# Program order on every engine, one unit of four head pairs per block, masks from iota, a joint update of r and k, and a weight conversion without GpSimd

## Chip, cores, metric

One core of one Trainium2 chip. The metric is the device time of one execution in microseconds (us), median of several; "span" is the time from the first to the last instruction of the profiled execution, some 2 us shorter. Engines: PE = TensorE, DVE = VectorE, ACT = ScalarE, POOL = GpSimd, SP = SyncE, which issues the DMAs.

## The reference

A recurrent attention (batch 4, 8 heads, 768 tokens, head size 48) and then an MLP with exact GELU over the 3072 tokens, model size 384, hidden size 2048. The MLP's weights come as float64.

```python
for t in range(S):                                   # rwkv6_finch
    kt, vt, rt, wt = k[:, :, t], v[:, :, t], r[:, :, t], w[:, :, t]
    cur = einsum('bhd,bhe->bhde', u[None] * kt, vt)
    y[:, :, t] = einsum('bhd,bhde->bhe', rt, state + cur)
    state = wt[..., None] * state + einsum('bhd,bhe->bhde', kt, vt)   # state starts at 0 for each batch
x = y.transpose(0, 2, 1, 3).reshape(3072, 384)
h = x @ w_in
out = (0.5 * h * (1 + erf(h / sqrt(2)))) @ w_out
```

## The kernel before

The tokens go in 8 blocks of 384 (two per batch). The attention of a block is split into 11 steps ("slots"): one product of r*u and k, six levels of products with an update of r and k after each, a transpose of k, the state, y from v, y from the state. Its result goes by ten small DMAs into `xT`, the input of the block's MLP. Attention of block x runs beside the MLP of block x-1, so only the first block's attention stands alone, and it stands beside the conversion of w_in from float64.

```python
def to_float32(dst, src):                    # one piece, 128 x 512 or 128 x 384; 28 pieces
    raw = cv.tile([128, PIECE], I64, name="raw", bufs=3)[:, 0:n]
    nc.sync.dma_start(out=raw, in_=src)
    ...
    nc.scalar.activation(out=f.bitcast(F32), in_=hi.bitcast(F32), func=AF.Abs)
    nc.vector.tensor_scalar(...)             # clamp
    nc.vector.tensor_scalar(...)             # shift and mask
    nc.vector.scalar_tensor_tensor(...)      # sign
    nc.vector.tensor_scalar(...)             # exponent of the low word
    nc.vector.scalar_tensor_tensor(...)      # low word, scaled
    nc.gpsimd.tensor_add(dst, f.bitcast(F32), e.bitcast(F32))

def attention(n):                            # n = block * 2 + unit; a unit is two head pairs
    ...
    before = st_of.get(n - UB)               # state of the block before
    ...
    for h in LEVELS:                         # 1, 2, 4, 8, 16, 32
        d = products(...)                    # PE; copied into a under a mask
        ...
        nc.vector.tensor_mul(r2, r2, t2[:, :, 0:1].to_broadcast([128, nb, h]))
        nc.gpsimd.tensor_mul(k2, k2, t2[:, :, 1:2].to_broadcast([128, nb, h]))
        nc.vector.tensor_mul(new, t2[:, :, 0], t2[:, :, 1])
        yield
    ...                                      # state: 11 small DVE instructions a unit (10 in a batch's second block)
    load(n + 2 * UB)

for x in range(NX):                          # no program-order line: the scheduler orders each engine
    slots = zip(*(attention(x * UB + i) for i in range(UB)))
    if x == 0:                               # beside the 12 pieces of w_in
        spread(slots, weights(in_pieces), len(in_pieces), len(in_pieces))
    else:                                    # beside the MLP before; x == 1 converts 16 pieces of w_out too
        ...
        spread(slots, steps, n, n - 4)
```

Of the kernel before, what the change touches and what calls it, by code (L numbers as in the profile page):

```python
# [10 lines left out]
U32 = mybir.dt.uint32  # L11
U8 = mybir.dt.uint8
# [5 lines left out]
C = 64  # L18
G = 64
T = 384  # L20
# [14 lines left out]
def kernel(  # L35
# [21 lines left out]

    nc = tc.nc
    NU = rkw.shape[0]
    D = 48  # L60
    NP = u.shape[1]
    UB = NP // Q
    N_TOK, DM = out.shape
    NX = N_TOK // T
# [8 lines left out]
    io = ctx.enter_context(tc.tile_pool(name="io", bufs=4))  # L73
# [3 lines left out]
    ps = ctx.enter_context(tc.tile_pool(name="ps", bufs=1, space=PSUM))  # L77

# [3 lines left out]
    def load(n):  # L82
        if n >= NU:
            return
        x = io.tile([128, 3, Q, T], F32, name="rkw_in")
        if n < UB:
            nc.sync.dma_start(out=x[:, 0:2], in_=rkw[n, :, 0:2])
            nc.sync.dma_start(out=x[:, 2], in_=rkw[n, :, 2])
        else:
            nc.sync.dma_start(out=x, in_=rkw[n])  # L90
        y = io.tile([128, v.shape[2]], F32, name="v_in")
        nc.sync.dma_start(out=y, in_=v[n])
        loaded[n] = x, y

    u_sb = const.tile([128, NP], F32, name="u_sb")
    nc.sync.dma_start(out=u_sb, in_=u)
    for n in range(UB):
        load(n)

    ident = const.tile([128, 128], F32, name="ident")  # L100
    make_identity(nc, ident)


    masks = {}

    def mask(h, n):
        masks[h] = const.tile([128, 1, n], U8, name=f"mask{h}")
        return wk.tile([128, n], F32, name="maskf")

    m = mask(0, C)  # L110
    for p in range(2):
        nc.vector.tensor_copy(out=m[half[p]], in_=ident[half[p], half[p]])
    nc.vector.tensor_copy(out=masks[0][:, 0, :], in_=m)
    for h in LEVELS[:-1]:
        m = mask(h, C // 2)
        for p in range(2):
            mv = m[half[p]].rearrange("p (q j) -> p q j", j=h)
            nc.gpsimd.memset(m[half[p]], 1.0)
            nc.gpsimd.affine_select(out=mv, in_=mv, compare_op=ALU.is_ge, fill=0.0, base=0,
                                    pattern=[[-2 * h, C // 2 // h], [0, h]], channel_multiplier=1)  # L120
            nc.gpsimd.affine_select(out=mv, in_=mv, compare_op=ALU.is_ge, fill=0.0, base=h - 1,
                                    pattern=[[2 * h, C // 2 // h], [0, h]], channel_multiplier=-1)
        nc.vector.tensor_copy(out=masks[h][:, 0, :], in_=m)


    a_bufs = [const.tile([128, 2, NI, C], F32, name=f"a{i}") for i in range(2)]
    for a in a_bufs:
        nc.gpsimd.memset(a, 0.0)

    st_bufs = [const.tile([128, Q * NC * D + G - D], F32, name=f"st{i}") for i in range(2 * UB)]  # L130
    for s in st_bufs:
        nc.gpsimd.memset(s, 0.0)

    w_in_sb = const.tile([128, NJ, DF], F32, name="w_in_sb")
    w_out_sb = const.tile([128, NF, DM], F32, name="w_out_sb")

    def to_float32(dst, src):

        n = src.shape[1]
        raw = cv.tile([128, PIECE], I64, name="raw", bufs=3)[:, 0:n]  # L140
        nc.sync.dma_start(out=raw, in_=src)
        words = raw.bitcast(U32).rearrange("p (a b) -> p a b", b=2)
        lo, hi = words[:, :, 0], words[:, :, 1]
        f = cv.tile([128, PIECE], U32, name="f")[:, 0:n]
        e = cv.tile([128, PIECE], U32, name="e")[:, 0:n]

        nc.scalar.activation(out=f.bitcast(F32), in_=hi.bitcast(F32), func=AF.Abs)  # L147
        nc.vector.tensor_scalar(out=f.bitcast(F32), in0=f.bitcast(F32), scalar1=as_float(0x38000000),  # L148
                                scalar2=as_float(0x47EFFFFF), op0=ALU.max, op1=ALU.min)
        nc.vector.tensor_scalar(out=f, in0=f, scalar1=3, scalar2=0x3FFFFFFF,  # L150
                                op0=ALU.logical_shift_left, op1=ALU.bitwise_and)

        nc.vector.scalar_tensor_tensor(out=f, in0=hi, scalar=0xC0000000, in1=f,  # L153
                                       op0=ALU.bitwise_and, op1=ALU.bitwise_or)

        nc.vector.tensor_scalar(out=e, in0=f, scalar1=0xFF800000, scalar2=None, op0=ALU.bitwise_and)  # L156
        nc.vector.scalar_tensor_tensor(out=e.bitcast(F32), in0=lo, scalar=2.0 ** -52, in1=e.bitcast(F32),  # L157
                                       op0=ALU.mult, op1=ALU.mult)
        nc.gpsimd.tensor_add(dst, f.bitcast(F32), e.bitcast(F32))  # L159

    def weights(pieces):
        for dst, src in pieces:
            if wide:
                to_float32(dst, src)
            else:
                nc.sync.dma_start(out=dst, in_=src)
            yield
# [4 lines left out]
    def attention(n):  # L172

        x, un = divmod(n, UB)
        first = x % HALVES == 0
        rkw_in, vt = loaded.pop(n)
        r, k, w = (rkw_in[:, i].rearrange("p q t -> p (q t)") for i in range(3))
        rc, kc = (z.rearrange("p (i c t) -> p i c t", c=2, t=C) for z in (r, k))
        at = a_bufs[n % 2]
        st = st_bufs[n % len(st_bufs)]  # L180
        before = st_of.get(n - UB)
        st_of[n] = st
# [4 lines left out]

        ru = wk.tile([128, Q * T], F32, name="ru")
        for q in range(Q):
            nc.scalar.activation(out=ru[:, q * T:(q + 1) * T], in_=r[:, q * T:(q + 1) * T], func=AF.Copy,  # L190
                                 scale=u_sb[:, un * Q + q:un * Q + q + 1])
        ruc = ru.rearrange("p (i c t) -> p i c t", c=2, t=C)

        def products(right, width):
            d = ps.tile([128, 2, BANK], F32, name="d", tag="d", bufs=3)
            for i in range(NI):
                for g in range(2):
                    for p in range(2):
                        nc.tensor.matmul(d[half[p], g, i * width:(i + 1) * width],  # L199
                                         lhsT=kc[half[g], i, p], rhs=right(half[g], i, p), start=True, stop=True)  # L200
            return d[:, :, 0:NI * width]

        d = products(lambda z, i, p: ruc[z, i, p], C)
        nc.vector.copy_predicated(out=at.rearrange("p g i t -> p (g i) t"),
                                  mask=masks[0].to_broadcast([128, 2 * NI, C]), data=d)
        yield

        tots = wk.tile([128, Q * T], F32, name="tots")
        tot, at_tot = w, 0
        for h in LEVELS:  # L210
            m = C // 2 // h
            right = rc.rearrange("p i c (m two j) -> p i c m two j", two=2, j=h)[:, :, :, :, 1, :]
            d = products(lambda z, i, p: right[z, i, p], C // 2)
            to = at.rearrange("p g i (m two j) -> p (g i) m two j", two=2, j=h)[:, :, :, 1, :]
            if m == 1:
                for p in range(2):
                    s = slice(p * 64, p * 64 + h)
                    nc.scalar.copy(out=at[s, :, :, h:], in_=d[s].rearrange("p g (i t) -> p g i t", t=h))
            else:
                nc.vector.copy_predicated(  # L220
                    out=to, mask=masks[h].rearrange("p o (q j) -> p o q j", j=h).to_broadcast([128, 2 * NI, m, h]),
                    data=d)
            nb = Q * T // (2 * h)
            t2 = tot.rearrange("p (n two) -> p n two", two=2)
            r2 = r.rearrange("p (n two j) -> p n two j", two=2, j=h)[:, :, 1, :]
            k2 = k.rearrange("p (n two j) -> p n two j", two=2, j=h)[:, :, 0, :]
            nc.vector.tensor_mul(r2, r2, t2[:, :, 0:1].to_broadcast([128, nb, h]))  # L227
            nc.gpsimd.tensor_mul(k2, k2, t2[:, :, 1:2].to_broadcast([128, nb, h]))  # L228
            new = tots[:, at_tot:at_tot + nb]
            nc.vector.tensor_mul(new, t2[:, :, 0], t2[:, :, 1])  # L230
            tot, at_tot = new, at_tot + nb
# [3 lines left out]
        kt_ps = ps.tile([128, 2, BANK], F32, name="kt_ps", tag="d", bufs=3)  # L235
        for i in range(NI):
            o = (i % N3) * 128
            nc.tensor.transpose(kt_ps[:, i // N3, o:o + 128], k[:, i * 128:(i + 1) * 128], ident)  # L238
        kt = wk.tile([128, NI, 2, G], F32, name="kt")
        nc.scalar.copy(out=kt.rearrange("p (b i) g d -> p b (i g d)", b=2), in_=kt_ps[:, :, 0:N3 * 128])  # L240
        yield

        vc = [[vt[:, (i * 2 + g) * D:(i * 2 + g) * D + G] for g in range(2)] for i in range(NI)]
        kv_ps = ps.tile([128, 2, BANK], F32, name="kv_ps", tag="d", bufs=3)
        for i in range(NI):
# [169 lines left out]
```

## Time and profile before

| before | value |
|---|---|
| time, median of 4 runs (range) | 740.7 us (739.8 to 742.0) |
| span, mean granted PE clock | 740.9 us, 0.968 |
| busy: PE, DVE, ACT, POOL | 679.4, 284.6, 137.9, 151.6 us |
| first MLP's last matmul ends | 183.5 us |
| from there to the end | 557.4 us |

PE is busy 92% of the span, and of the missing 8% all but 3.4 us at the very end lie before 183.5 us (the stretches are in the prediction). What PE waits for there is the list of PE's waits, kernel before (columns: what waited, for what; total us, times, longest):

```profile
PE d L199 <- DVE rkw_in L227: 19.7, 10, 7.5
PE y_ps L268 <- DVE st L259: 16.8, 1, 16.8
PE d L199 <- ACT ru L190: 8.5, 2, 7.9
PE d L199 <- issue: 7.5, 1, 7.5
```

To be seen: DVE's updates (`rkw_in`) and DVE's state (`st`) hold PE for 36.5 us. I shall split every kernel at one place, the end of the first MLP's last matmul: **head** before it, **rest** after it.

### The profile page before, as it was taken

The numbers are of one execution on the slowest core, as the hardware profiler recorded it, in microseconds if no ns is written. First come the engines' busy times: TensorE is split into PE (matmuls) and PEld (weight loads), VectorE is DVE, ScalarE is ACT, GpSimd is POOL, SyncE is SP. The second block draws the span as 40 slices with busy tenths as digits, with TensorE's granted clock in tenths as the row PEclk, the third lists the DMA queues.
The fourth block names the chain that finished last, engine by engine and source line by source line (L and its number), as shares of the span: only waits on it lengthen the run. The fifth ranks groups of instructions, "written<-read, shape, count | busy, mean of one in ns | idle before, by whom it ended". The sixth has DMA issues, their size and how long they took to land.

```text
span 740.9 us, 20544 instructions
## 1 busy us (share of the span) xinstructions
PE 679.4 (92%) x9296; PEld 444.6 (60%) x9296; DVE 284.6 (38%) x644; ACT 137.9 (19%) x254; POOL 151.6 (20%) x166
## 2 busy tenths in 40 slices
PE   3733697899999999999999999999999999999998
PEld 2632454466666666666666666666666666665554
DVE  2999969941433034231433035121433044200000
ACT  2122232401222021301121021301120011201200
POOL 5643435400231013200330014100330023100000
PEclk9985698999999999999999999999999999999999
DMA  8145723215000510024000500033000100010000
GB/s 344 66 132 160 245 65 107 87 46 175 8 3 2 157 71 2 3 77 150 2 3 28 169 32 3 2 123 104 3 2 13 43 13 3 2 43 22 0 12 21
DMA packets 16966, 47.06 MB, mean 64 GB/s; under 512 B 2800, under 2 KB 8944, under 8 KB 15088
## 3 DMA queue, kind: packets, MB, share of 16 engines
q1 hardware_dynamic: 16880, 45.76, 18.6%
q8 instruction: 73, 1.20, 0.7%
q14 instruction: 13, 0.11, 0.0%
HBM read 36.31 MB, written 4.72 MB: 55 GB/s over the span
## 4 chain that ended last, share of the span: by engine, by line
PE 84%; DVE 10%; DMA 3%; issue 2%; POOL 1%; ACT 0%; SPq 0%; POOLq 0%; DVEq 0%
PE o_ps L320 34%; PE h_ps L311 33%; PE d L199 10%; PE y_ps L284 3%; DVE rkw_in L227 2%; DVE f L153 2%; DMA v_in<-in_v_dram 2%; PE y_ps L268 1%; PE kv_ps L248 1%; DVE f L148 1%; DVE e L156 1%; DVE e L157 1%; PE kt_ps L238 1%; DVE f L150 1%; DMA rkw_in<-in_rkw_dram 1%
## 5 line engine op out<-in xcount | busy, mean ns | idle before, releaser
L311 PE MATMUL h_ps<-xT,w_in_sb 128*128 128x384 f32 x768 | 266.0, 499 | 2.0 <-DMA xT<-ysb 2.0
L320 PE MATMUL o_ps<-w_out_sb,gt 128*128 128x384 f32 x768 | 256.4, 491 | 2.1 <-ACT gt L314 2.1
L320 PEld LDWEIGHTS o_ps<-w_out_sb,gt 128*128 128x128 f32 x768 | 144.3, 191 | 98.9 <-ACT gt L314 2.3
L311 PEld LDWEIGHTS h_ps<-xT,w_in_sb 128*128 128x128 f32 x768 | 143.5, 192 | 94.8 <-issue 3.0
L228 POOL TENSOR_TENSOR rkw_in<-rkw_in,tots 128x384 f32<-128x384 f32 x80 | 83.7, 1063 | 135.2 <-PE d L199 131.6
L199 PEld LDWEIGHTS d<-rkw_in 64*64 64x64 f32 x4608 | 82.2, 148 | 46.0 <-issue 26.4
L314 ACT ACTIVATE gt<-h_ps 128x384 f32<-128x384 f32 x128 | 62.6, 490 | 251.0 <-PE h_ps L311 251.0
L199 PE MATMUL d<-rkw_in 64*64 64x32 f32 x4608 | 88.3, 231 | 20.2 <-DVE rkw_in L227 19.7
L325 DVE COPY o_sb<-o_ps 128x384 f32<-128x384 f32 x24 | 13.4, 558 | 228.1 <-PE o_ps L320 228.1
L220 DVE COPY_PREDICATED a<-mask,d 128x384 f32<-128x384 uint8 x80 | 59.9, 749 | 102.0 <-PE d L199 101.7
L228 POOL TENSOR_TENSOR rkw_in<-rkw_in 128x384 f32<-128x384 f32 x16 | 21.0, 1333 | 294.6 <-PE d L199 294.6
L227 DVE TENSOR_TENSOR rkw_in<-rkw_in,tots 128x384 f32<-128x384 f32 x80 | 67.3, 841 | 31.1 <-PE d L199 30.2
L259 DVE SCALAR_TENSOR_TENSOR st<-st,tots,kv_ps 128x48 f32<-128x48 f32 x160 | 30.0, 259 | 33.3 <-PE kv_ps L248 33.2
L287 ACT COPY ysb<-y_ps 128x768 f32<-128x768 f32 x16 | 12.8, 797 | 142.7 <-PE y_ps L284 142.7
L190 ACT ACTIVATE ru<-rkw_in,u_sb 128x384 f32<-128x384 f32 x32 | 17.4, 604 | 93.1 <-PE d L199 78.8
L199 PE MATMUL d<-ru,rkw_in 64*64 64x64 f32 x768 | 15.8, 239 | 16.1 <-ACT ru L190 8.5
L268 PE MATMUL y_ps<-a,v_in 64*64 64x64 f32 x768 | 13.8, 226 | 16.8 <-DVE st L259 16.8
L147 ACT ACTIVATE f<-raw 128x384 f32<-128x384 f32 (+1 forms) x28 | 17.0, 608 | 56.8 <-POOL w_out_sb L159 29.7
L284 PEld LDWEIGHTS y_ps<-rkw_in,st 64*64 64x64 f32 x752 | 24.5, 144 | 4.1 <-issue 3.8
L153 DVE SCALAR_TENSOR_TENSOR f<-raw,f 128x384 uint32<-128x384 uint32 (+1 forms) x28 | 26.1, 931 | 0.2
L199 PEld LDWEIGHTS d<-ru,rkw_in 64*64 64x64 f32 x768 | 14.3, 151 | 19.7 <-issue 10.9
L284 PE MATMUL y_ps<-rkw_in,st 64*64 64x64 f32 x752 | 25.6, 229 | 0.1
(35 smaller groups left out, 259.9 us busy)
## 6 DMA issues: line engine op xcount, KB each, us to landing
rkw_in<-in_rkw_dram SPq DMA_DIRECT2D x14, 1152.0 KB, 6.2
raw<-in_w_in_dram SPq DMA_DIRECT2D x12, 512.0 KB, 3.7
raw<-in_w_out_dram SPq DMA_DIRECT2D x16, 384.0 KB, 3.0
v_in<-in_v_dram SPq DMA_DIRECT2D x16, 296.0 KB, 4.3
out_dram<-o_sb SPq DMA_DIRECT2D x24, 192.0 KB, 2.0
xT<-ysb SPq DMA_DIRECT2D x48, 72.0 KB, 3.2
rkw_in<-in_rkw_dram SPq DMA_DIRECT2D x2, 768.0 KB, 5.7
rkw_in<-in_rkw_dram SPq DMA_DIRECT2D x2, 384.0 KB, 6.1
```

The source lines that it names most:

```text
L153: nc.vector.scalar_tensor_tensor(out=f, in0=hi, scalar=0xC0000000, in1=f, op0=ALU.bitwise_and, op1=ALU.bitwise_or)
L190: nc.scalar.activation(out=ru[:, q * T:(q + 1) * T], in_=r[:, q * T:(q + 1) * T], func=AF.Copy, scale=u_sb[:, un * Q + q:un * Q + q + 1])
L199: nc.tensor.matmul(d[half[p], g, i * width:(i + 1) * width], lhsT=kc[half[g], i, p], rhs=right(half[g], i, p), start=True, stop=True)
L220: nc.vector.copy_predicated(out=to, mask=masks[h].rearrange("p o (q j) -> p o q j", j=h).to_broadcast([128, 2 * NI, m, h]), data=d)
L227: nc.vector.tensor_mul(r2, r2, t2[:, :, 0:1].to_broadcast([128, nb, h]))
L228: nc.gpsimd.tensor_mul(k2, k2, t2[:, :, 1:2].to_broadcast([128, nb, h]))
L259: nc.vector.scalar_tensor_tensor(out=stq[:, q, c], in0=stq[:, q, c - 1] if c else b4[:, q, NC - 1], scalar=totq[:, q, c:c + 1], in1=kvq[:, ...
L268: nc.tensor.matmul(y_ps[half[g], p, i * C:(i + 1) * C], lhsT=vc[i][g][half[p]], rhs=at[half[p], g, i, :], start=(i == 0), stop=True, skip_ ...
L284: nc.tensor.matmul(y_ps[half[g], c % 2, i * C:(i + 1) * C], lhsT=src[half[g], o:o + G], rhs=rc[half[g], i, c % 2], start=False, stop=True, ...
L311: nc.tensor.matmul(h_ps, lhsT=w_in_sb[:, j, f * 128:(f + 1) * 128], rhs=xT[:, j, :], start=(j == 0), stop=(j == NJ - 1))
L314: nc.scalar.activation(out=gt, in_=h_ps, func=AF.Gelu)
L320: nc.tensor.matmul(o_ps, lhsT=gs[f][:, i * 128:(i + 1) * 128], rhs=w_out_sb[:, f, :], start=(f == 0), stop=(f == NF - 1))
```

## The change

Its intent: keep DVE free of the work that delays the first block. GpSimd is taken out of the conversion and of the k update, because DVE instructions took longer beside its adds (one and the same conversion instruction took 0.41 us at 42.29, and 1.34 at 48.63, beside an add from 48.01 to 49.68 us); masks come from two iota and a few integer instructions; the four head pairs are one unit from block 2 on, so instructions are half as many and twice as wide; conversions are placed by hand (three before the state, the other 25 in the first MLP's stage); every engine keeps the source's order; loads are issued when their block is next but one.

```diff
+    ctx.enter_context(tc.manual_schedule(engines=None))     # program order on all engines
...
-        nc.gpsimd.affine_select(...)  # two per mask half, ten halves
+    nc.gpsimd.iota(row, pattern=[[0, C]], base=0, channel_multiplier=1)
+    nc.gpsimd.iota(col, pattern=[[1, C]], base=0, channel_multiplier=0)
+        nc.vector.tensor_scalar(out=s_h, in0=row[:, 0:C // 2], scalar1=sh, ..., op0=ALU.logical_shift_right)
+        nc.vector.tensor_scalar(out=m_h, in0=col[:, 0:C // 2], ...)
+        nc.vector.tensor_tensor(out=masks[h][:, 0, :], in0=s_h, in1=m_h, op=ALU.is_equal)
...
     def to_float32(dst, raw):
+        nc.scalar.activation(out=e.bitcast(F32), in_=lo, func=AF.Identity, scale=2.0 ** -51, bias=two)
         nc.scalar.activation(out=f.bitcast(F32), in_=hi.bitcast(F32), func=AF.Abs)
         nc.vector.tensor_scalar(...)  # clamp, as before
-        (shift and mask; sign; exponent; low word: four DVE instructions; add on GpSimd)
+        nc.vector.tensor_scalar(out=f, in0=f, scalar1=3, scalar2=None, op0=ALU.logical_shift_left)
+        nc.vector.scalar_tensor_tensor(out=e, in0=hi, scalar=0x80000000, in1=e,
+                                       op0=ALU.bitwise_and, op1=ALU.bitwise_or)
+        nc.vector.tensor_tensor(out=dst.bitcast(U32), in0=f, in1=e, op=ALU.add)
...
-        before = st_of.get(n - UB)
+        before = None if first else st_bufs[(x - 1) % 2]
...
-            nc.vector.tensor_mul(r2, r2, t2[:, :, 0:1].to_broadcast([128, nb, h]))
-            nc.gpsimd.tensor_mul(k2, k2, t2[:, :, 1:2].to_broadcast([128, nb, h]))
+            rk = bass.AP(...)          # r's odd halves and k's even halves in one pattern
+            nc.vector.tensor_mul(rk, rk, tt)
...
+    slots = zip(*(attention(0, unit) for unit in range(units_of(0))))
+    for slot, _ in enumerate(slots, 1):
+        if slot == N_SLOTS - 3:
+            convert(NJ)
+    load_rkw(2)
+    load_v(2)
+    for x in range(1, NX):
+        lead, last = (12, N_STEPS - 2) if x == 1 else (0, N_STEPS - 4)
+        place = [lead + (last - lead) * i // (N_SLOTS - 1) for i in range(N_SLOTS)]
+        slots = attention(x, 0)
+        for step, _ in enumerate(mlp(x - 1)):
+            while x == 1 and converted[0] < len(pieces) and (converted[0] - NJ) * 3 < (step + 1) * 4:
+                convert()
+            while place and place[0] <= step:
+                place.pop(0)
+                next(slots)
+        load_rkw(x + 2)
+        load_v(x + 2)
```

In the kernel before, PE also multiplies the first 64 tokens of a batch with a state slot of the batch before. Read in the code, that slot holds zeros: the second block of a batch fills its slots 0 to 4, and slot 5, which these products read, keeps the zeros it was set to at the start.

## The prediction

> **What bounds the kernel now.** I read three views in this order: the chain that ended last (where the bound changes), a table of stretches cut at those places, and the order of time and the groups of instructions inside the stretches that are not bound by TensorE. A "stage" below is one block of 384 tokens: its attention runs beside the MLP of the block before.
>
> First the stretches; columns are length, busy time of each engine, granted clock, DMA share and GB/s.
>
> ```profile
> 0.00:90.00 90.00, 40.88 (x1211) 36.94 (x1211) 75.32 (x143) 21.70 (x33) 45.79 (x70) 0.81 0.54 190
> 90.00:183.50 93.50, 84.56 (x915) 51.94 (x914) 57.95 (x138) 20.83 (x41) 26.52 (x25) 0.93 0.31 99
> 183.50:265.50 82.00, 82.00 (x1169) 53.21 (x1168) 25.47 (x63) 14.95 (x28) 13.27 (x12) 1.00 0.16 52
> 593.50:675.50 82.00, 82.00 (x1166) 53.49 (x1166) 22.66 (x49) 12.81 (x24) 13.26 (x12) 1.00 0.05 16
> 675.50:740.90 65.40, 61.99 (x193) 36.20 (x191) 2.23 (x4) 7.84 (x16) 0.00 (x0) 1.00 0.03 12
> ```
>
> To be seen: from 183.5 us on, PE is busy for all of each 82.0 us stage; six such stages and a last MLP make 6 x 82.0 + 65.4 = 557.4 us. No engine but PE can shorten that. Only the first 90 us (no MLP yet) and the next 93.5 us (the first MLP, 11.5 us over a full stage) can give: at best 90 + 11.5.
>
> Then what DVE does in the first 90 us, where it is busy for 75 us:
>
> ```profile
> 18.43 0.18 DVE L123 CAST mask<-maskf 128x32 uint8<-128x32 f32 x1 [0.42 <-POOL maskf L121]
> ...
> 48.63 1.34 DVE L156 TENSOR_SCALAR e<-f 128x512 uint32<-128x512 uint32 x1
> 49.88 0.25 DVE L259 SCALAR_TENSOR_TENSOR st<-st,tots,kv_ps 128x48 f32<-128x48 f32 x1
> 50.06 0.68 DVE L157 SCALAR_TENSOR_TENSOR e<-raw,e 128x512 f32<-128x512 uint32 x1
> 50.66 0.41 DVE L148 TENSOR_SCALAR f<-f 128x512 f32<-128x512 f32 x1
> 51.00 0.25 DVE L259 SCALAR_TENSOR_TENSOR st<-st,tots,kv_ps 128x48 f32<-128x48 f32 x1
> 51.17 1.33 DVE L150 TENSOR_SCALAR f<-f 128x512 uint32<-128x512 uint32 x1
> ...
> 58.64 1.60 DVE L153 SCALAR_TENSOR_TENSOR f<-raw,f 128x512 uint32<-128x512 uint32 x1
> ...
> 68.41 1.13 DVE L259 SCALAR_TENSOR_TENSOR st<-st,tots,kv_ps 128x48 f32<-128x48 f32 x6
> ```
>
> To be seen: masks come from GpSimd until 18 us though the first data is there at 6. The state recurrence, 22 small instructions, takes from 44 to 69.5 us because a conversion of w_in sits between any two steps; at the end six run in 1.13 us. The same conversion instruction takes 0.41 or 1.34 us, 0.68 or 1.60: it is held up.
>
> [...] the 1.60 us one above starts beside a GpSimd add (58.29 to 59.69 us) and ends 0.55 us after it. [...] The trace: 0.54 us for 384 contiguous elements, 0.72 at pair distance 1. [...] The trace: the 96 products of a level take 2.95 us in the first 40 us, 1.53 us in a full stage.
>
> **The change part by part.** In the built program PE has the same matmuls as before, so the PE floor stays. I use undisturbed durations of the trace, start to start where instructions follow each other.
>
> 1. Start. [...] the 17 little DVE mask instructions (about 0.15 each, as small ones in the trace) end near 10; the tot products (0.56 + 1.31 = 1.9) end at 12.2. Level 1 of both units: joint update 2 x 1.3 (768 elements at the 0.72/384 rate), copies 4 x 0.9, the second tots 1.9: 8.1, to 20.3. Level 2: 2 x 1.2 + 2 x 0.9 = 4.2, to 24.5. Three levels at about 3.1 [...], to 33.8; the last update 1.8, to 35.6. Transpose and copy of both units [...] to 38.8. Before, this point was at 42.
>
> 2. Three pieces of w_in stand in front of the state now. ScalarE's two passes (0.6 each) put the first at 40; a piece costs DVE, by starts, 0.34 + 0.34 + 0.60 and an integer add. No row shows that add; I take it as a SCALAR_TENSOR_TENSOR, 0.6. That is 1.9, up to 2.1 where one needs the result of the one before (in the trace 0.40 instead of 0.27 to the next): 2.0. So to 46.2. State 2 x 2.1 to 50.4, fences, y 2 x 2.0 [...] to 54.8, copy to 55.7, ten xT issues at 0.65 begin at 53.8, landing 2 us later: **first MLP complete in xT at 62** instead of 83.4, and PE no longer stands behind other work until 90. Gain 28 us.
>
> 3. But 25 of 28 pieces are left, where 15 were. Order on ScalarE puts the first behind the first gelu: DVE starts at 62.4 + 3 = 65.4. Up to the update of level 8, DVE has 9 pieces x 2.0 and 14 of w_out x 1.63 (0.27 + 0.27 + 0.47 + 0.5, between 1.5 and 1.77) = 40.8; tots of four units 2.6, update of 1536 elements 2.6, copies 3.6; level 2 4.1; level 4 2.6; update of level 8 1.7: 58.0 together. PE in that time has about 45 us, so **DVE sets the pace** and the point is 123.4. Then in program order about 7 us until step 19 of 28, and 30.2 us of PE that nothing hides: 8 steps x 2.68 = 21.4 and the products, transpose, kv, y and y again at 1.5 + 1.3 + 1.5 + 1.5 + 2.9.
>
> 4. The last attention step stands after step 26, so only one step (2.7 us) covers the way of y into xT, which needs about 8 (copy, ten issues, landing): 5.3 us idle. **Second MLP at 123.4 + 7 + 30.2 + 5.3 = 165.9**, before 185 (183.5 with the products that stood first). Of the 28 us, nine have been given back.
>
> 5. Full stages. GpSimd's k update (1.08 us, 12 a stage) goes into DVE, 25 us busy there, which has room. Program order costs twice: the products with u wait for ru, which stands behind the first gelu (0.6), and the second level waits for a PSUM buffer that four copies release (0.5): estimated 1.2 a stage, 7 in six. The xT way has 3 steps (8.0 us) and needs about 8: no margin. Merging level 1 with u saves next to nothing.
>
> Sum: 165.9 + 492 + 7 + 65.4 = **730 us**.
>
> **The rivals.** (a) *PE-bound stage 1.* If the conversions cost less than I think, the stage shrinks toward 82 + 5 us, and without the 1.2 us in the full stages: 62 + 87 + 492 + 65 = 706. For it: the GpSimd collisions go, 0.5 to 0.9 us each. Against it: DVE needs 58 us before PE's last 37 whatever happens to collisions, as I have already used free durations. (b) *Nothing is gained.* [...] For it: the narrow 8 us[...]. Against it: in the old stage the xT issues (7.3 us for ten) share the queue with a 1.18 MB load issued ahead; the new one issues loads after. (c) *DMA becomes the bound of stage 1.* A load of 2.96 MB for block 2 stands before the raw pieces; at 400 GB/s (seen between 5 and 20 us) it ends about 67, and the next piece is wanted at 72. If it slips, 3 to 5 us more.
>
> **Range and chances.** The start is uncertain by about 5 us, the DVE pace of stage 1 by 8, the full stages by 6: together 11, so 714 to 743, a bit wider below, as the order was evidently arranged on purpose (where attention begins in stage 1). Faster by 2% means under 725.4: 0.36. Within: 0.58. Slower: 0.06.
>
> **What would show it right or wrong.** First h_ps matmul at 57 to 67; state instructions in one run of about 4.5 us; DVE nearly always busy from 65 to 130 with PE waiting for it; a PE idle of 4 to 6 us for xT before the second MLP at 160 to 171; stages of 83 us with two short waits, for ru and for a copy. Wrong if the stages are 82.0 or above 85, if stage 1 shows PE full, if the add differs from 0.6 us, or if iota ends after 10 us.

The sum came to 730 us, and terms of it are cut: in step 1 a term for GpSimd's start, which the "near 10" still holds (the 17 mask instructions are 2.6 us of it), so that all later times hold it too. With three parentheses a cause went that no trace shows; their figures are of the kernel before's trace: 2.95 us for 96 products (beside 2 x 0.9 + 2 x 0.5 of DVE) in the levels at 3.1, 2 x 1.5 and 0.8 for transpose and copy, 2 x 2.0 for y (78 products in 4.43 us from 70.26). The 1.3 and 2.6 us of the joint updates are an estimate, scaled from 0.72 us for 384 elements (DVE's update of r, L227). Rival (b) came to some 755.

## The result, and the profile after

728.0 us (727.8 to 728.2, 4 runs) against 740.7: ratio 0.9827, 95% interval 0.981 to 0.9844, so 1.7% faster, inside the 2%. Ratios here are the mean time of one kernel's runs over the mean of the other's in the same rounds, so not quite the ratio of the medians that are quoted.

The stretches of the kernel after, cut where its bound changes (columns as in the prediction):

```profile
0.00:54.40 54.40, 31.78 (x957) 29.98 (x957) 37.85 (x90) 13.66 (x20) 4.48 (x11) 0.90 0.49 180
54.40:160.50 106.10, 92.73 (x1165) 57.24 (x1165) 70.66 (x149) 42.49 (x78) 0.00 (x0) 0.90 0.38 124
165.90:251.70 85.80, 81.74 (x1143) 53.48 (x1143) 24.15 (x44) 14.83 (x28) 0.00 (x0) 0.96 0.12 44
415.30:660.80 245.50, 245.50 (x3478) 159.82 (x3477) 80.43 (x149) 44.50 (x84) 0.00 (x0) 1.00 0.12 40
660.80:726.00 65.20, 61.90 (x192) 36.11 (x191) 2.23 (x4) 7.84 (x16) 0.00 (x0) 1.00 0.04 12
```

To be seen: the first block's attention takes 54.4 us where 90 stood, and the first MLP's stage 106.1 where 93.5 stood. The cuts are not quite alike: here the cut is at the first `h_ps` matmul (first product of an MLP), which in the kernel before started at 78.9 us; cut there, the kernel before has 78.9 + 104.6. Later stages are full of PE again, 245.5 / 3 = 81.8 us each, but the second MLP's stage has lost 4 us of PE and has a clock of 0.96. In head and rest: 160.4 + 565.6 us, against 183.5 + 557.4. **The head gained 23.1 us, the rest gave 8.2 back.**

Where the head's gain comes from, in DVE's order of time, kernel after:

```profile
42.17 0.68 DVE L205 SCALAR_TENSOR_TENSOR e<-raw,e 128x512 uint32<-128x512 uint32 x1
42.89 0.69 DVE L207 CUSTOM_DVE_ANT_0 w_in_sb<-f,e 128x1024 uint16<-128x1024 uint16 x1
43.50 0.25 DVE L322 COPY st<-kv_ps 128x96 f32<-128x96 f32 x1
43.78 1.84 DVE L327 SCALAR_TENSOR_TENSOR st<-st,tot_sb,kv_ps 128x48 f32<-128x48 f32 x10
45.54 0.25 DVE L322 COPY st<-kv_ps 128x96 f32<-128x96 f32 x1
45.82 1.84 DVE L327 SCALAR_TENSOR_TENSOR st<-st,tot_sb,kv_ps 128x48 f32<-128x48 f32 x10
47.58 0.22 DVE L343 COPY fence<-y_ps 128x2 f32<-128x2 f32 x2
62.43 0.43 DVE L202 TENSOR_SCALAR f<-f 128x512 f32<-128x512 f32 x1 [14.64 <-ACT f L201]
```

To be seen: the state, which took from 44 to 69.5 us before, now runs in one piece from 43.5 to 47.6. The uint16 line is the integer add. Then DVE has nothing to do for 14.64 us, because its next conversion waits for a ScalarE pass that stands behind the first gelu function.

Where the rest lost it, in PE's order of time, kernel after (in brackets: idle time before the line, and what ended it):

```profile
157.59 2.85 PE L391 MATMUL o_ps<-w_out_sb,gt 128*128 128x384 f32 x8
160.50 0.88 PE L382 MATMUL h_ps<-xT,w_in_sb 128*128 128x384 f32 x2
162.84 0.91 PE L382 MATMUL h_ps<-xT,w_in_sb 128*128 128x384 f32 x2 [1.46 <-DMA xT<-ysb]
165.12 0.88 PE L382 MATMUL h_ps<-xT,w_in_sb 128*128 128x384 f32 x2 [1.37 <-DMA xT<-ysb]
165.93 1.60 PE L254 MATMUL d<-rkw_in 64*64 64x32 f32 x96
167.35 0.78 PE L254 MATMUL d<-ru_sb,rkw_in 64*64 64x64 f32 x37
172.19 1.97 PE L254 MATMUL d<-ru_sb,rkw_in 64*64 64x64 f32 x59 [4.06 <-issue]
```

To be seen: two waits for `xT`, which the prediction has, and 4.06 us of "issue" in the middle of 96 equal products, which it hasn't. "issue" is time in which PE waited for nothing the profile shows. A load of 2.4 MB and one of 0.6 MB had been issued at 164.1 and 164.6 us. PE's 59 products after it take 1.97 us, where 96 take 1.61 in an undisturbed stage.

### The profile page after: what moved, and what is told of

The parts are those of the page before. It is cut to its first block, busy times and chain, and to the rows that moved or that the text cites. A ratio compares the mean times of both kernels' runs of the same rounds, so it can differ in the third digit from the quotient of the medians.

```text
span 726.0 us, 19903 instructions
## 1 busy us (share of the span) xinstructions
PE 679.7 (94%) x9248; PEld 443.8 (61%) x9248; DVE 272.1 (37%) x542; ACT 153.0 (21%) x282; POOL 4.5 (1%) x11
## 3 DMA queue, kind: packets, MB, share of 16 engines
q8 instruction: 72, 1.18, 0.7%
## 4 chain that ended last, share of the span: by engine, by line
PE 84%; DVE 10%; issue 2%; SPq 2%; DMA 1%; ACT 1%; ACTq 0%; DVEq 0%
PE o_ps L391 34%; PE h_ps L382 32%; PE d L254 11%; PE y_ps L358 3%; DVE e L205 2%; PE kt_ps L296 2%; PE y_ps L339 2%; PE kv_ps L312 1%; SPq L369 1%; DVE f L204 1%; DVE rkw_in L271 1%; DVE f L202 1%; DVE w_in_sb L207 1%; DVE w_out_sb L207 1%; DMA u_sb<-in_u_dram 1%
## 5 line engine op out<-in xcount | busy, mean ns | idle before, releaser
L271 DVE TENSOR_TENSOR rkw_in<-rkw_in,tot_sb 128x1536 f32<-128x1536 f32 (+1 forms) x45 | 71.1, 1580 | 93.7 <-PE d L254 93.6
L254 PEld LDWEIGHTS d<-rkw_in 64*64 64x64 f32 x4608 | 80.2, 146 | 38.8 <-issue 19.3
L280 DVE COPY_PREDICATED a_sb<-mask,d 128x384 f32<-128x384 uint8 x80 | 55.0, 747 | 0.0
L327 DVE SCALAR_TENSOR_TENSOR st<-st,tot_sb,kv_ps 128x48 f32<-128x48 f32 x160 | 29.0, 258 | 0.3
L254 PE MATMUL d<-ru_sb,rkw_in 64*64 64x64 f32 x768 | 17.8, 253 | 9.9 <-ACT ru_sb L234 5.0
L278 ACT COPY a_sb<-d 32x384 f32<-32x384 f32 x32 | 15.0, 469 | 38.5 <-PE d L254 37.9
L271 DVE TENSOR_TENSOR rkw_in<-rkw_in 128x1536 f32<-128x1536 f32 (+1 forms) x9 | 14.2, 1581 | 23.2 <-PE d L254 23.2
L254 PEld LDWEIGHTS d<-ru_sb,rkw_in 64*64 64x64 f32 x768 | 16.1, 162 | 10.7 <-issue 5.2
L199 ACT ACTIVATE e<-raw,two 128x384 f32<-128x384 uint32 (+1 forms) x28 | 19.6, 699 | 9.5 <-DVE w_out_sb L207 5.1
L339 PE MATMUL y_ps<-a_sb,v_in 64*64 64x64 f32 x768 | 13.8, 226 | 7.6 <-DVE st L327 7.6
L339 PEld LDWEIGHTS y_ps<-a_sb,v_in 64*64 64x64 f32 x768 | 12.6, 140 | 11.5 <-issue 11.5
```

Source lines behind the costliest of these rows:

```text
L199: nc.scalar.activation(out=e.bitcast(F32), in_=lo, func=AF.Identity, scale=2.0 ** -51, bias=two)
L254: nc.tensor.matmul(d[half[p], g, n * width:(n + 1) * width], lhsT=kc[half[g], b, i, p], rhs=right(half[g], b, i, p), start=True, stop=True)
L271: nc.vector.tensor_mul(rk, rk, tt)
L278: nc.scalar.copy(out=at[s, b, :, :, h:], in_=db[s].rearrange("p g (i t) -> p g i t", t=h))
L280: nc.vector.copy_predicated(out=at[:, b].rearrange("p g i (m two j) -> p (g i) m two j", two=2, j=h)[:, :, :, 1, :], mask=masks[h].rearran ...
L327: nc.vector.scalar_tensor_tensor(out=stq[:, qb + q, c], in0=stq[:, qb + q, c - 1] if c else b4[:, qb + q, NC - 1], scalar=totq[:, b * Q + ...
```

## The experiments

Twelve runs; the kernel before ran in each of the three batches (741.6, 742.0 and 742.4 us). All outputs are right. Times are medians.

| run | program order on | time | ratio to before | span = head + rest |
|---|---|---|---|---|
| before | none | 740.7 | 1 | 740.9 = 183.5 + 557.4 |
| b_fix | none | 741.5 | 0.9999 | 737.9 = 182.0 + 555.9 |
| b_order | all | 767.7 | 1.0345 | 766.3 = 209.0 + 557.3 |
| after | all | 728.0 | 0.9827 | 726.0 = 160.4 + 565.6 |
| a_auto | none | 705.8 | 0.9513 | 705.2 = 136.1 + 569.1 |
| a_oldconv | all | 760.7 | 1.0262 | 760.1 = 193.7 + 566.4 |
| a_kpool | all | 733.7 | 0.9892 | 729.8 = 164.0 + 565.8 |
| a_convlate | all | 723.6 | 0.9755 | 720.9 = 156.7 + 564.2 |
| a_last24 | all | 719.1 | 0.9693 | 717.6 = 161.7 + 555.9 |
| a_loadlate | all | 728.6 | 0.9815 | 727.3 = 161.3 + 566.0 |
| o_pe | PE | 721.5 | 0.9722 | 725.1 = 147.1 + 578.0 |
| o_da | DVE, ACT | 716.7 | 0.9651 | 714.7 = 152.8 + 561.9 |
| a_tie | all | 725.0 | 0.9766 | 722.3 = 160.9 + 561.4 |
| auto_tie | none | 694.5 | 0.9347 | 690.8 = 134.4 + 556.4 |

Each split is that of one profiled execution: of o_pe it was the slowest run (726.9 us), of a_kpool, b_fix and auto_tie the fastest. Where the head's order was not changed, the heads agree within 1.7 us: 160.4, 161.3 and 160.9 (after, a_loadlate, a_tie), 136.1 and 134.4 (a_auto, auto_tie), 183.5 and 182.0 (before, b_fix). Smaller differences between heads say nothing.

My theory at the start: the gain is the conversion and the state running in one piece, and program order moves the time by little. The rival was that program order is needed for the gain. Both are in the expectation of a_auto.

**a_auto: the change without program order.**

```diff
-    ctx.enter_context(tc.manual_schedule(engines=None))
```

> The changed kernel with the scheduler in charge again (the line that asks for program order is taken out); all else is as in the changed kernel. Theory: the gain is from what is left out of the start (10 of 13 conversions, the waits for GpSimd), not from program order as such. The scheduler's order in the built program of the start is nearly the same and keeps the state steps together, so 722 to 738 us. Rival: program order is the gain; then it falls back toward the kernel before, over 738.

705.8 us: below what the theory (722 to 738) and the rival (over 738) allowed. Both fall: program order does not carry the gain, it costs 22 us. The first MLP on PE, first in the kernel after, then in a_auto:

```profile
59.03 13.20 PE L382 MATMUL h_ps<-xT,w_in_sb 128*128 128x384 f32 x32 [0.54 <-DMA xT<-ysb]
72.79 6.37 PE L382 MATMUL h_ps<-xT,w_in_sb 128*128 128x384 f32 x18 [0.55 <-ACT gt L385]
80.52 2.20 PE L382 MATMUL h_ps<-xT,w_in_sb 128*128 128x384 f32 x6 [1.36 <-ACT gt L385]
```

```profile
55.31 25.14 PE L381 MATMUL h_ps<-xT,w_in_sb 128*128 128x384 f32 x76 [0.88 <-DMA xT<-ysb]
80.39 1.60 PE L253 MATMUL d<-rkw_in 64*64 64x32 f32 x96
```

To be seen: left to the scheduler, PE does 76 of these without a break; in program order it stops for gelu functions (`gt`) that stand behind conversion passes on ScalarE. The scheduler starts conversions at 32 us, between DVE's other work, and puts the next block's first products in front of the MLP.

**b_order: program order alone, on the kernel before.**

```diff
+    ctx.enter_context(tc.manual_schedule(engines=None))
```

> The kernel before with the one line that keeps program order on all engines, nothing else. In the kernel after, leaving that line out gained 22 us. Theory A: program order by itself costs wherever the source puts slow conversion work in one lump, so here too it costs, and more, because the old conversion (3.7 us a piece) stands in front of the first gelu functions: 750 to 775 us against 740. Rival: the source of the kernel before was ordered for a scheduler that follows it closely, and the order on the engines hardly moves: 738 to 745. If it is faster than 738, program order was a gain of the change and only the place of the new conversions lost it.

767.7 us, +26, all of it in the head (209.0 against 183.5). That program order costs here too agrees with theory A; where it costs does so only in part. PE's longest waits in b_order:

```profile
PE d L201 <- POOL rkw_in L230: 35.1, 9, 16.6
PE d L201 <- ACT ru L192: 26.0, 3, 17.4
```

In the first block, each level's k update on GpSimd now stands behind the addition of a w_in piece; PE waits up to 16.6 us for it, and its last product of y from the state ends at 83.9 us, in the kernel before at 74.8. Then ScalarE's first pass for the next block (`ru`) stands behind a conversion pass that itself waits 15.4 us for its raw piece; PE waits 17.4 us in one piece for it. The first `h_ps` matmul starts at 104.1 us instead of 78.9, and from there to the end of the head both kernels take 105 us. So the whole loss lies before the first gelu function. Program order costs in both sources, 22 and 26 us.

**a_oldconv: the change with the old conversion.**

```diff
     def to_float32(dst, raw):
-        (two ScalarE passes, four DVE instructions, the last an integer add)
+        (one ScalarE pass, five DVE instructions, and nc.gpsimd.tensor_add)
```

> The changed kernel with the conversion of the kernel before (five DVE instructions and a GpSimd add in place of four, one ScalarE pass fewer). Theory: DVE paces the first MLP stage (from 62.4 us it is busy without a break up to 128), so its fifth instruction (0.35 to 0.41, by starts) and blocked ones (about 0.5 a piece) count in full for 25 pieces: 10 to 25 us slower than the changed kernel, 738 to 753. Rival: ScalarE paces it, with two passes and gelu; one pass fewer, so no slower, 722 to 730.

760.7 us, 32.6 above the kernel after, all in the head. The direction is as expected, the size was too small. DVE's order of time there:

```profile
67.93 0.42 DVE L200 TENSOR_SCALAR f<-f 128x512 f32<-128x512 f32 x1
68.38 1.40 DVE L202 TENSOR_SCALAR f<-f 128x512 uint32<-128x512 uint32 x1
69.82 0.69 DVE L204 SCALAR_TENSOR_TENSOR f<-raw,f 128x512 uint32<-128x512 uint32 x1
```

The 1.40 us instruction takes 0.43 when undisturbed (at 65.67); a GpSimd add runs from 68.09 to 69.50. A piece takes DVE 3.7 us (67.93 to 71.61) instead of 2.1; 25 pieces at 1.6 more would be 40 us at most (16 of them are smaller), and 33 show. With program order, this conversion would have made the change a loss.

**a_kpool: the k update back on GpSimd.**

```diff
-            nc.vector.tensor_mul(rk, rk, tt)
+            nc.vector.tensor_mul(r2, r2, t2)
+            nc.gpsimd.tensor_mul(k2, k2, t2k)
```

> The changed kernel with the k update on GpSimd again, apart from r. Theory: in the full stages nothing changes (PE is full). In the first MLP stage DVE loses six times half of 1.66, 5 us, but GpSimd takes 1536/384 x ... half the elements at about 2 us for 768 and holds the next level's products; in the start each level waits for 2 us on GpSimd instead of 0.9 on DVE. Sum: between 3 us faster and 8 us slower, I expect 3 slower (731). Rival: the joint update is what makes the start short; then over 8 us slower.

733.7 us, 5.7 above the kernel after, inside the expectation and a little over its guess. By the medians the joint update is worth that. GpSimd took 0.91 to 1.18 us for one update of 384 elements in the first block, and 2.44 to 2.46 for two in a row; the "about 2 us for 768" was an estimate, near twice the 1.08 us of the kernel before.

**b_fix: the kernel before, without the products with the slot of the batch before.**

```diff
-        before = st_of.get(n - UB)
+        before = None if first else st_of.get(n - UB)
```

> The kernel before, with one word of the change alone: a batch's first block takes no state of the batch before. The trace of the kernel before has 752 matmuls of the second y group, that of the changed kernel 704, so 48 are dropped, 16 in each of three full stages, which PE fills completely (2.94 us for 96, 2.48 for 80). Theory: 3 x 0.49 = 1.5 us faster than the kernel before (ratio 0.998), and the error against the reference falls, by my own reckoning in float64 from about 6 per cent to rounding. Rival: these stages are held by something beside PE, then no gain at all.

741.5 us, ratio 0.9999 (0.9985 to 1.0013): no gain in the time. Its trace has stages of 82.0 and 81.5 us by turns where the kernel before has 82.0, so some 1.5 us in three stages may be there; the times don't show them. Not settled, and small.

**a_convlate: where do the 22 us of program order lie?** Three conversions behind the state instead of ahead of it, four more directly after the first block.

```diff
-        if slot == N_SLOTS - 3:
+        if slot == N_SLOTS - 1:
             convert(NJ)
+    convert(4)
...
-            while x == 1 and ... and (converted[0] - NJ) * 3 < (step + 1) * 4:
+            while x == 1 and ... and (converted[0] - NJ - 4) * 3 < (step + 1) * 4:
```

> The kernel after, still in program order, with the first three conversions issued after the state instead of ahead of it, and four more conversions issued directly after the first block. Theory A (the 22 us of program order are idle VectorE time: 14.6 us in which its next conversion waits for a ScalarE pass behind the first gelu function): the idle stretch goes, the level-8 update of the second block and all behind it come about 13 us sooner: 712 to 718 us. Rival (the loss is in the order of the products and the gelu functions, not in this gap): 722 us or more, though the gap is gone.

723.6 us: 4.4 gained where theory A had at least 10; the rival's number holds. The 14.64 us gap is gone, and other waits take its place: PE waits 8.5 us for the first weights and later 6.9 us for a gelu function, in front of which ScalarE waits for a raw piece:

```profile
ACT e L199 <- DMA raw<-in_w_in_dram: 7.0, 2, 6.1
```

That piece is issued at 60.4 us, behind the 3 MB of block 3's loads issued at 55.4: rival (c) of the prediction, met here at 6.1 us. So an idle DVE was not by itself the price of program order.

**o_pe and o_da: which engine's order costs?** The program-order line takes a set of engines.

```diff
-    ctx.enter_context(tc.manual_schedule(engines=None))
+    ctx.enter_context(tc.manual_schedule(engines={mybir.EngineType.PE}))                                  # o_pe
+    ctx.enter_context(tc.manual_schedule(engines={mybir.EngineType.DVE, mybir.EngineType.Activation}))    # o_da
```

> The kernel after with program order on TensorE only; the scheduler orders ScalarE, VectorE and the DMA queue. With all engines in program order it took 728, with none 706. Theory P (the 22 us are lost because TensorE's own order puts products that must wait for VectorE ahead of first-MLP products that could run): 720 us or more, PE's waits for the second block's updates stay. Rival V (they are lost because conversions stand behind gelu functions on ScalarE and VectorE): 710 us or less.

> The mirror of it: program order on VectorE and ScalarE only, the scheduler orders TensorE and the DMA queue. Theory P: 712 us or less. Rival V: 718 us or more, with VectorE's wait of about 14 us for the ScalarE pass behind the first gelu still there. If both this run and its mirror lie between 712 and 720, each order takes part of it.

721.5 (717.8 to 726.9, the widest of all) and 716.7 us. By the times theory P would hold for o_pe and neither for o_da; but the times mix two things. In o_pe 10.2 us are four issue waits at stage starts (3.80, 2.01, 1.97, 2.46), a matter of the next runs. The heads are free of them (one trace each): 136.1 with no order, 147.1 with PE's, 152.8 with DVE's and ScalarE's, 160.4 with all. PE's order costs 11.0 us, DVE's and ScalarE's 16.7, together a bit more than the 24.3 of all. Each takes part, as the third outcome of the expectation said, though its bounds for the times did not hold. The traces show two ways. In o_da it is the wait of the kernel after (14.64 us there) for the ScalarE pass behind the first gelu function, in DVE's list:

```profile
DVE f L202 <- ACT f L201: 18.7, 2, 15.0
```

In o_pe, PE's order puts the second block's first products behind 78 matmuls of the MLP, at 77.75 us; in a_auto they begin at 46.0. So the updates on DVE start later, and PE waits for one of them:

```profile
77.75 1.60 PE L254 MATMUL d<-rkw_in 64*64 64x32 f32 x96
87.75 2.79 PE L254 MATMUL d<-rkw_in 64*64 64x32 f32 x96 [4.83 <-DVE rkw_in L271]
```

**a_last24: the second block's steps two steps earlier.**

```diff
-        lead, last = (12, N_STEPS - 2) if x == 1 else (0, N_STEPS - 4)
+        lead, last = (12, N_STEPS - 4) if x == 1 else (0, N_STEPS - 4)
```

> The kernel after with the second block's steps placed two steps earlier in the stage of the first MLP, so that its y copies do not end behind the MLP's last products. Theory: the waits for the second xT (1.46 + 1.37 us) shrink and nothing takes their place: 724 to 727 us. Rival: the steps are held by the conversions on VectorE anyway, PE meets the level-8 update sooner and waits there: 728 us or more.

719.1 us, 8.9 gained where 1 to 4 were expected. Head 161.7 (1.3 longer), rest 555.9, 9.7 shorter. Between 160 and 180 us PE is now busy for 20.00 us at clock 1.00, against 13.05 us at 0.83 in the kernel after. The 9.7 are 1.46 + 1.37 of xT waits, the 4.06 of issue, and 2.8 (what is left) of slower matmuls behind them. A short wait was cheap in the list and dear in what followed it. Why the 4.06 us went as well, though the load was issued at 162.75 us, beside the same products, this run does not show.

**a_loadlate: the bulk load seven steps later in the source.**

```diff
+            if x == 2 and step == 6:
+                load_rkw(3)
+                load_v(3)
...
-        load_rkw(x + 2)
-        load_v(x + 2)
+        if x != 1:
+            load_rkw(x + 2)
+            load_v(x + 2)
```

> The kernel after with the loads of the fourth block (2.4 MB and 0.6 MB) issued seven steps later. Theory B: PE's 4.06 us of issue wait at 168.1 us come from the bulk load issued at 164.1 us[...]: the wait goes or moves to the new place of the load. If it moves along, the time stays within 1 us of 728; if it is smaller there, up to 4 us are gained. Rival (the wait belongs to the place in PE's program[...]): it stays at the same products, 4 us long, and the time is 728.

728.6 us; but the experiment did not do what it was to do. The load was issued at 164.95 us, where the kernel after has 164.13: in SyncE's order of time it follows the issue of an output at 164.32 us, with no wait between the two. The issue wait was 1.23 us this time, at the same product (after 37 of 96), and still the rest is as long (566.0 us): PE is busy for 3.2 us more (558.4 against 555.2). So the length of this wait does not tell its cost. Beyond that the run shows only that a line's place did not time the load.

**a_tie and auto_tie: the same with a dependency.** One column of the load's buffer is first written by ScalarE from the 14th gelu result of the stage, so the load can't start sooner.

```diff
+            if after is not None:
+                nc.scalar.copy(out=t[:, 0:1], in_=after[:, 0:1])
             nc.sync.dma_start(out=t, in_=rkw[x])          # v likewise
...
+            if x > 1 and step == 13:
+                load_rkw(x + 1, gt)
+                load_v(x + 1, gt)
...
-        load_rkw(x + 2)
-        load_v(x + 2)
```

> The kernel after with the loads of block x+1 really held back until the 14th gelu function of the stage of block x (a one-column ScalarE write of that function's result into the load's buffer comes first, so that the load cannot start sooner); moving the lines alone had left the load where it was. So no bulk load runs during the products at a stage's start. Theory B (PE's issue wait of 4.06 us behind the second MLP's start comes from the bulk load beside it): the wait is under 1 us, the time 723 to 726 us. Rival: it stays at 1 to 4 us, 727 to 729 us.

> The same held-back loads in the version without the program-order line (706 us), in which PE has three issue waits of about 2 us, each some 8 us after a bulk load was issued at a stage's start. Theory B: those three go, 699 to 701 us. Rival: they stay, 705 to 707 us.

a_tie: 725.0 us, as theory B had it. The load is issued at 206.8 us instead of 164.1, and PE has no issue wait after 24 us. The two waits for `xT` are still there, and the matmuls behind them are slow without any load:

```profile
163.27 0.91 PE L386 MATMUL h_ps<-xT,w_in_sb 128*128 128x384 f32 x2 [1.49 <-DMA xT<-ysb]
165.62 1.62 PE L386 MATMUL h_ps<-xT,w_in_sb 128*128 128x384 f32 x2 [1.43 <-DMA xT<-ysb]
167.16 2.79 PE L258 MATMUL d<-rkw_in 64*64 64x32 f32 x96
```

The granted clock from 160 to 180 us was 0.83 (1.00 in a_last24). From these single traces the 9.7 us of a_last24 can be parted: some 4.2 go with the load (rests of 565.6 and 561.4), and 5.5 with the waits for `xT` (561.4 and 555.9), of which the waits themselves are 2.9 and slower matmuls 2.5.

auto_tie: 694.5 us, better than theory B's 699 to 701. PE's order of time at a stage's start, first in a_auto (load issued at 218.09), then in auto_tie (257.81):

```profile
221.83 1.60 PE L253 MATMUL d<-rkw_in 64*64 64x32 f32 x96
223.25 0.79 PE L253 MATMUL d<-ru_sb,rkw_in 64*64 64x64 f32 x40
226.05 1.04 PE L253 MATMUL d<-ru_sb,rkw_in 64*64 64x64 f32 x56 [2.01 <-issue]
227.02 5.83 PE L381 MATMUL h_ps<-xT,w_in_sb 128*128 128x384 f32 x12
```

```profile
220.00 1.60 PE L257 MATMUL d<-rkw_in 64*64 64x32 f32 x96
221.43 1.61 PE L257 MATMUL d<-ru_sb,rkw_in 64*64 64x64 f32 x96
222.96 4.14 PE L385 MATMUL h_ps<-xT,w_in_sb 128*128 128x384 f32 x12
```

To be seen: the wait is gone, and also the 12 matmuls behind it take 4.14 instead of 5.83 us, the rate of an undisturbed stage. The granted clock from 226 to 233 us in a_auto was 0.76; in auto_tie it was 1.00 from 217 to 231. One such stage costs 2.01 + 1.69 = 3.7 us, three 11.1. The traces' rests differ by 12.7 (569.1 and 556.4), of which three waits are 6.0 and longer busy time of PE 5.9; the medians differ by 11.3, while a_auto's own runs lie from 702.5 to 707.5. I had counted the waits alone.

What waits? No trace shows it. That the bulk load takes part in the wait is shown by a_tie and auto_tie: with the loads moved, the wait of 4.06 us (kernel after) and the three of 6.0 us together (a_auto) are gone. It is not enough by itself: the kernel after issues loads of the same size at 253.0, 335.0, 416.4 and 498.3 us, and has no issue wait there. The wait breaks a row of equal products at the same product (after 37 of 96) in the kernel after, a_loadlate and a_convlate (after 36 in a_oldconv, 32 in a_kpool). That a place in PE's program and a load beside it have to meet would fit both; it stays a guess of mine.

## Why the prediction was right

The time was predicted at 730 us and came out at 728.0, within 2% of the kernel before as said. The mechanism of the head held (the state in one run, then DVE as the pace); that of the full stages did not. By its steps:

- **The PE floor.** "The same matmuls" was not so: 48 records fewer. Worth at most 1.5 us (b_fix).
- **Step 1, start.** Right in its end, wrong in its parts. The first block's last update ended at 33.3 us instead of 35.6. No wait for GpSimd's start appeared: iota ran at 0.83 us for 0.18, and the mask instructions ended at 6.2. The joint update of 768 elements took 0.96 us at every level, not 1.3. Instead three of the mask instructions were held up about 1 us each beside GpSimd's memsets of 1.07 to 4.6 us (DVE at 1.04 us: 1.46; in a_auto the same one comes after the memsets, at 8.08 us, and takes 0.19). Why the early products are slow (2.95 us for 96) is not shown: the clock column reads 1.00 from 20 to 40 us in the kernel before, and 0.59 in a_auto, where 322 of them take 9.21 us, 2.75 for 96. By its own terms (35.6, 2 x 1.5, 0.8) the step ends at 39.4, not 38.8; a slip without effect.
- **Step 2, the state ahead.** The integer add of 512 words was 0.69 us long (a SCALAR_TENSOR_TENSOR of that size 0.68; with 384 words 0.56 and 0.55) and 0.61 from start to start (taken as 0.6), the conversion 2.1 a piece (2.0), the state 4.1 us in one run (4.2). The first xT was complete at 59.0 instead of 62. This was the gain, as named.
- **Step 3, DVE sets the pace.** DVE was busy without a break from 62.4 to 128.5, after the idle stretch in front of it, and the level-8 update ended at 121.5 (predicted 123.4). The best step: it began 3.0 us sooner than predicted and took 59.1 us instead of 58.0. What it left unsaid is that this pace was itself the work of program order. With the scheduler the same instructions start at 32 us, and the head is 24 us shorter. I had booked order as 1.2 us a stage in the full stages, where it cost nothing, and not in the head, where it cost 24.
- **Step 4, the xT wait.** Two waits of 2.8 us together, not 5.3, and the second MLP complete at 165.1 (predicted 165.9). The step did not see what follows such a wait: 4.06 us of issue and slow matmuls. a_last24 and a_tie show all of it to be worth 9.7 us.
- **Step 5, full stages.** 7 us were predicted for ru and for the PSUM buffer. They did not come: 81.8 us a stage, PE full. The level-1 update of 1536 elements took 1.75 us, not 2.6, which fits buffers that come free in time. By the prediction's own list ("wrong if the stages are 82.0") this step failed.

So the sum was right partly by cancelling: the 7 us of step 5 were not there, and about 7 us (4.06 and the slow matmuls) stood at the second MLP's start unforeseen. **Rivals.** (a), a first stage bound by PE, is near what a_auto is, reached by the scheduler's order and not by cheaper conversions; that its 706 us is a_auto's time is luck (its rest was put at 557 and is 569.1). (b), a loss, needed the old conversion (a_oldconv, 760.7, where it had 755). (c), the DMA as bound, showed only in a_convlate.

Where the expected gain went, then: into program order, which takes back 22 us of it, and into waits at the start of stages. With the order left to the scheduler and the bulk loads held back, auto_tie is 33.5 us faster than the kernel after and 6.5% faster than the kernel before; it is the best version here. a_last24's edit on top of it was not tried. Nor were the masks from iota, the wide units and the places of the loads taken out alone. The conversion (32.6), the joint update (5.7) and program order (-22.2) make 16.1 of the 12.7 us measured, so the others can't have brought much, if effects add, which no run shows.

## What to carry to other kernels

Fixing the order by hand is a part of a change like any other and can be taken out in one line or for one engine at a time: do so before the order is credited with anything. A wait of 1 to 2 us on the bounding engine cost about twice what the list of waits says, as PE then ran slower (2.01 + 1.69 us in a_auto, 2.9 + 2.5 in a_tie), so remove short waits in an otherwise full stretch first. To keep a bulk load away from a stretch, give it a true dependency; a later line in the source moved nothing where the queue had nothing else to wait for (issued at 164.95 us against 164.13).
